# The first loads of x in contiguous rows, the first half block in two parts, and column pairs in the blocks of the first column quarter

## The chip, the core and the metric

The kernel runs on one NeuronCore of a Trainium2 chip. Its engines work side by side and are tied by semaphores: TensorE (PE) multiplies matrices, VectorE (DVE), ScalarE (ACT) and GpSimd (POOL) do elementwise work, and SyncE (SP) issues DMA transfers; ScalarE and GpSimd can issue some too. Sixteen DMA engines move the data. The metric is the device time of one execution in microseconds (us).

## The reference

Only the first of two sublayers matters here. `x` is 2048 x 512, the two sequence matrices are 2048 x 2048, all in float32.

```python
h = _layernorm(x, axis=-1) * (1 + ca) + sa
a = jnp.einsum("bsd,ed->bse", h, dft_hid_re)
b = jnp.einsum("bsd,ed->bse", h, dft_hid_im)
y = jnp.einsum("ts,bse->bte", dft_seq_re, a) - jnp.einsum("ts,bse->bte", dft_seq_im, b)
x = x + ga * y
```

The second sublayer (a gated MLP with a 2048 x 2048 spatial matrix `w_sp`) follows, and takes the rest of the time.

## The kernel before

**What is multiplied first.** The kernel begins with products of the sequence matrices (`cr`, `ci`) and the normalised rows of `x`. A matrix is taken in blocks of 512 x 512 (`quad`); `src` lists the 32 blocks in the order of use. A block has to be turned before TensorE can contract over its columns. It is loaded into a tile `stage[b]`, 128 partitions x 16 x 128, in four transfers, one for each 32 partitions (`load_block`), and VectorE turns it by 32 x 32 squares in four instructions (`squares`, k = 0 to 3), each of which gives a tile `t` of 128 x 512.

**Steps.** Step n = 4b + k uses turn k of block b and one row block of `x` (128 of its rows; rows "X[0]" to "X[3]" go with block 0). Products are made in pieces of high and low part: `ah` (ScalarE's rounded copy of `t`) and `al` (VectorE's difference `t` - `ah`) on one side, `hh` and `hl` of the normalised row on the other. A step is three groups of four matmuls: `ah` x `hh`, `al` x `hh`, `ah` x `hl`. Step 0 is an exception: four plain float32 matmuls of `t` with the whole normalised row `xn` (L543). `prep_hi` makes `t` and `ah`, `prep_lo` makes `al`; in the steady part `t` is made three steps ahead and `al` two.

**The rows of x.** `stats_first` makes mean and variance on VectorE (BN_STATS, BN_AGGR, an add), then GpSimd makes the power -1/2 and the product of mean and scale (for row 0 VectorE makes the product, L445). ScalarE then normalises: `whole_first` for row 0, `hi_first` for rows 1 to 3 (`hh`), `norm_x` once more for `xn`, from which VectorE subtracts `hh` (`lo_h`, L525).

**The order of the work** is written out by hand at the end of the function: every engine takes its instructions in the order of the code. The loads at the start are row 0 in four transfers (two queues, `two`), the first half of block 0 (columns 0 to 63 of each group of 128) in four, row 1 in four, rows 2 and 3 in four, the second half of block 0 in four, then block 1 and the next rows.

**Completion semaphores.** Each transfer that SyncE or ScalarE issues takes the next of eight completion semaphores (DMAHW0 to DMAHW7 in the rows of the order below), and its issue waits until the transfer that had this semaphore eight places before has landed. So at most eight are under way, and a queue that waits at one issue holds back all that stand behind it.

## Time and profile before

| | before |
|---|---|
| time, median of 3 runs (lowest to highest) | 931.72 us (931.36 to 932.32) |
| profiled execution: its time; its span | 931.77 us; 930.0 us |
| TensorE busy | 924.2 us, 99% of the span |
| VectorE, ScalarE, GpSimd busy | 738.2, 409.1, 199.1 us |
| TensorE's granted clock, mean | 0.999 |

The span goes from the first to the last instruction of the profiled execution; the time of the same execution is 1.77 us longer. A granted clock of 1 is full speed. An engine counts as busy while one of its instructions runs; waiting and issuing transfers don't count.

### The profile page before, as it was taken

How to read it: one execution, taken by the hardware profiler on the slowest of the kernel's cores; microseconds unless marked ns; L12 is line 12 of the kernel's file. 1: busy time of each engine (PE TensorE's matmuls, PEld its weight loads, DVE VectorE, ACT ScalarE, POOL GpSimd, SP SyncE). 2: the span in 40 equal slices, each digit the busy share in tenths (PEclk: the TensorE clock that was granted, in tenths of full speed). 3: DMA queues.
4: the chain of work that ended last, by engine and by line, in shares of the span. 5: the costliest groups of instructions: out<-in, count | busy, mean ns of one | idle time of the engine just before them, and what ended most of it. 6: DMA issues, size and time to landing. Idle time of an engine off the chain costs nothing.

```text
span 930.0 us, 12339 instructions
## 1 busy us (share of the span) xinstructions
PE 924.2 (99%) x4053; PEld 760.4 (82%) x4053; DVE 738.2 (79%) x1218; ACT 409.1 (44%) x733; POOL 199.1 (21%) x375
## 2 busy tenths in 40 slices
PE   9999999999999999999999999999999999999998
PEld 5888888888888888888888888888888888888887
DVE  7799968787687677875678788899799789986762
ACT  5694424232132222322577877674544544331121
POOL 2330000224554165323512321331000000000000
PEclk9999999999999999999999999999999999999999
DMA  9995762856639977996463864444464566734651
GB/s 218 225 227 118 142 158 46 193 147 171 158 91 319 283 220 217 275 343 227 141 217 130 279 201 103 118 105 105 105 146 102 130 142 143 178 97 149 185 178 57
DMA packets 246976, 157.88 MB, mean 170 GB/s; under 512 B 140384, under 2 KB 214368, under 8 KB 246784
## 3 DMA queue, kind: packets, MB, share of 16 engines
q1 hardware_dynamic: 233248, 119.57, 52.2%
q0 software_dynamic: 12272, 36.86, 11.4%
q8 instruction: 32, 0.52, 0.2%
q10 hardware_dynamic: 1392, 0.66, 0.2%
q14 instruction: 32, 0.26, 0.1%
HBM read 120.33 MB, written 36.71 MB: 169 GB/s over the span
## 4 chain that ended last, share of the span: by engine, by line
PE 98%; DMA 1%; SPq 0%; ACTq 0%; DVE 0%; ACT 0%; issue 0%; DVEq 0%
PE gp L99 12%; PE gp L97 12%; PE gp L98 12%; PE gw L99 10%; PE gw L97 10%; PE gw L98 10%; PE yp L99 3%; PE yp L98 3%; PE yp L97 3%; PE op L98 3%; PE op L97 3%; PE op L99 3%; PE fp L98 1%; PE fp L97 1%; PE fp L99 1%; PE z2s L98 1%
## 5 line engine op out<-in xcount | busy, mean ns | idle before, releaser
L269 ACT ACTIVATE ah<-t 128x512 fp32r<-128x512 f32 x235 | 148.5, 632 | 362.6 <-DVE t L190 242.7
L287 DVE TENSOR_TENSOR al<-t,ah 128x512 fp32r<-128x512 f32 x235 | 160.6, 683 | 55.7 <-PE gp L98 30.9
L98 PE MATMUL gp<-al,hh 128*128 128x512 f32 x496 | 193.0, 389 | 0.0
L97 PE MATMUL gp<-ah,hh 128*128 128x512 f32 x496 | 193.0, 389 | 0.0
L99 PE MATMUL gp<-ah,hl 128*128 128x512 f32 x496 | 193.0, 389 | 0.0
L190 DVE STREAM_TRANSPOSE t<-stage 128x512 f32<-128x512 f32 x236 | 165.5, 702 | 6.3 <-DMA stage<-in_A_dft_seq_re_dram 3.1
L98 PE MATMUL gw<-al,bh 128*128 128x512 f32 x400 | 155.6, 389 | 0.0
L99 PE MATMUL gw<-ah,bl 128*128 128x512 f32 x384 | 149.5, 389 | 0.0
L97 PE MATMUL gw<-ah,bh 128*128 128x512 f32 x384 | 149.4, 389 | 0.0
L98 PEld LDWEIGHTS gp<-al,hh 128*128 128x128 f32 x496 | 93.1, 188 | 19.5 <-DVE al L287 0.2
L97 PEld LDWEIGHTS gp<-ah,hh 128*128 128x128 f32 x496 | 93.1, 188 | 19.4
L99 PEld LDWEIGHTS gp<-ah,hl 128*128 128x128 f32 x496 | 93.1, 188 | 19.3
L98 PEld LDWEIGHTS gw<-al,bh 128*128 128x128 f32 x400 | 75.1, 188 | 15.7
L99 PEld LDWEIGHTS gw<-ah,bl 128*128 128x128 f32 x384 | 72.1, 188 | 15.3 <-DVE bl L948 0.3
L97 PEld LDWEIGHTS gw<-ah,bh 128*128 128x128 f32 x384 | 72.1, 188 | 14.9
L920 POOL DMA_DIRECT2D s_d<-sj x64 | 35.1, 548 | 107.2 <-DVE sj L912 82.3
L97 PE MATMUL yp<-hth,gh 128*128 128x512 f32 x128 | 49.8, 389 | 0.0
L98 PE MATMUL yp<-htl,gh 128*128 128x512 f32 x128 | 49.8, 389 | 0.0
L99 PE MATMUL yp<-hth,gl 128*128 128x512 f32 x128 | 49.8, 389 | 0.0
L665 POOL DMA_DIRECT2D ht_d<-hturn x62 | 41.0, 667 | 23.1 <-DVE hturn L661 18.2
L97 PE MATMUL op<-woh,uh 128*128 128x512 f32 x110 | 42.8, 389 | 0.0
L98 PE MATMUL op<-wol,uh 128*128 128x512 f32 x110 | 42.8, 389 | 0.0
(247 smaller groups left out, 1449.4 us busy)
## 6 DMA issues: line engine op xcount, KB each, us to landing
stage<-in_A_dft_seq_im_dram SPq DMA_DIRECT2D x64, 256.0 KB, 6.0
sj<-in_B_w_sp_dram SPq DMA_DIRECT2D x32, 512.0 KB, 7.2
s_d<-sj POOLq DMA_DIRECT2D x64, 256.0 KB, 4.7
stage<-s_d SPq DMA_DIRECT2D x128, 128.0 KB, 2.9
stage<-in_A_dft_seq_re_dram SPq DMA_DIRECT2D x60, 256.0 KB, 5.6
stage<-in_B_w_sp_dram SPq DMA_DIRECT2D x88, 128.0 KB, 3.0
wm<-in_w_mod_dram SPq DMA_DIRECT2D x16, 256.0 KB, 6.1
xr<-in_A_x_dram POOLq DMA_DIRECT2D x16, 256.0 KB, 4.5
```

What stands on the lines that cost most here:

```text
L97: nc.tensor.matmul(acc, ah, bh, start=first, stop=False, skip_group_check=go_on)
L98: nc.tensor.matmul(acc, ah, bl, start=False, stop=False, skip_group_check=go_on)
L99: nc.tensor.matmul(acc, al, bh, start=False, stop=last, skip_group_check=go_on)
L190: nc.vector.transpose(dst.rearrange("p (b i) -> p b i", i=32), block[:, :, 32 * k:32 * k + 32])
L269: nc.scalar.activation(AH[n], T[n], AF.Copy)
L287: nc.vector.tensor_tensor(AL[n], t, AH[n].bitcast(F32), op=ALU.subtract)
L665: eng.dma_start(v[a, i], ht[32 * a:32 * a + 32].rearrange("c (b r) -> c b r", r=32))
L920: nc.gpsimd.dma_start(s_d[m, r, g][b * P:(b + 1) * P, :], a)
```

## The change

Row blocks 0 and 1 now are the first 256 rows of `x` (each group of 32 partitions has 64 rows running), and row blocks 2 and 3 are the next 256, two neighbouring rows for each partition, so that they come in one transfer of 128 x 1024. The blocks of the first column quarter of `cr` and `ci` (eight of the 32, `SRC_G` 0) are loaded to match: `load_pairs` takes 64 columns at a time, so each of these blocks but the first takes eight transfers where it took four, in runs of 64 elements where there were 128. `turn_dft` turns k = 0 and 1 as before; for k = 2 and 3 it reads every second element, since the columns of the two row blocks alternate.

The first half of block 0 comes in two parts, twelve squares and four squares, each in four transfers, and is turned for step 0 in the same two parts. Both parts stand ahead of row 1, of which ScalarE issues one transfer, after its table load and first activation, and SyncE three. The normalising of row 0 and the high part of row 1 are made in halves of 256 columns. GpSimd makes row 0's product of mean and scale. VectorE takes the statistics of row 1 ahead of the turn for step 1.

```diff
@@ -133,11 +133,12 @@
     def quad(a, r, k):
         return a[r * Q:(r + 1) * Q, k * Q:(k + 1) * Q]
 
-    src = []
+    src, SRC_G = [], []
     for t in range(NQ):
         for g, j in ([(g, j) for g in range(NQ) for j in range(2)] if t == 0 else
                      [(g, j) for j in range(2) for g in range(NQ)]):
             src.append(quad((cr, ci)[j], t, g))
+            SRC_G.append(g)
     N2 = 4 * len(src)
     N1 = N2 + 8
     YPROD = (6, 7, 4, 5, 3)
@@ -160,12 +161,31 @@
         for q in range(4):
             engs[q].dma_start(tile_[32 * q:32 * q + 32], v[q][:, :, 64 * h:64 * h + 64])
 
+    def load_pairs(tile_, a, h, engs=(nc.sync,) * 4, bs=slice(0, 16)):
+
+        v = a.rearrange("(b j) (h a s) -> h a j b s", j=32, a=4, h=2)
+        for q in range(4):
+            engs[q].dma_start(tile_[32 * q:32 * q + 32, bs, 64 * h:64 * h + 64], v[h, q][:, bs, :])
+
+    def turn_dft(n, block, k, bs=slice(0, 16)):
+
+        t = T[n].rearrange("p (b i) -> p b i", i=32)
+        if SRC_G[n // 4] or k < 2:
+            nc.vector.transpose(t[:, bs, :], block[:, bs, 32 * k:32 * k + 32])
+        else:
+            v = block.rearrange("p b (h i c) -> p b h i c", h=2, c=2)
+            nc.vector.transpose(t[:, bs, :], v[:, bs, 1, :, k - 2])
+
     XB = []
 
     def load(b):
         if b < len(src):
             stage[b] = blocks.tile([P, 16, P], F32, tag="stage", bufs=2, name=f"stage{b}")
-            load_block(stage[b], src[b])
+            if SRC_G[b]:
+                load_block(stage[b], src[b])
+            else:
+                for h in range(2):
+                    load_pairs(stage[b], src[b], h)
         elif b < len(src) + 2:
             j = b - len(src)
             XB.append(blocks.tile([P, 4, Q], F32, tag="stage", bufs=2, name=f"xb{j}"))
@@ -264,7 +284,7 @@
             elif n >= N4:
                 squares(T[n], stage[b][:, k % 2], k // 2)
             else:
-                squares(T[n], stage[b], k)
+                turn_dft(n, stage[b], k)
         AH[n] = SE[2][:, n - N4] if N4 <= n < N4 + 4 else blocks.tile([P, Q], F32R, tag="ah", bufs=4, name=f"ah{n}")
         nc.scalar.activation(AH[n], T[n], AF.Copy)
         if not N2 <= n < N4 and k == 3:
@@ -365,8 +385,8 @@
     def keep_busy(n, k):
 
         ps = bank(k, "busyp")
-        for _ in range(n):
-            nc.tensor.matmul(ps, ones, busy, start=True, stop=True)
+        for w in n:
+            nc.tensor.matmul(ps[:, :w], ones, busy[:, :w], start=True, stop=True)
 
     def fold_sum(t, w, u):
 
@@ -419,14 +439,18 @@
 
     X, XG, LN, NRM, h_hi, h_lo = {}, {}, {}, {}, {}, {}
 
-    def load_x(g, ks=range(4), eng=nc.sync):
+    def load_x(g, ks=range(4), engs=(nc.sync,) * 4):
 
         if g not in XG:
             XG[g] = spool.tile([P, 4, D], F32, tag="x", bufs=2, name=f"x{g}")
         k0, k1 = ks[0], ks[-1] + 1
-        v = x.rearrange("(g a k i) d -> g a i k d", g=NQ, a=4, i=32)
-        for a in range(4):
-            eng.dma_start(XG[g][32 * a:32 * a + 32, k0:k1, :], v[g, a][:, k0:k1, :])
+        if not g and k0 == 2:
+            nc.sync.dma_start(XG[g][:, 2:, :], x[2 * P:Q, :].rearrange("(p k) d -> p k d", k=2))
+        else:
+            v = (x.rearrange("(g a k i) d -> g a i k d", g=NQ, a=4, i=32)[g] if g else
+                 x[:2 * P, :].rearrange("(a k i) d -> a i k d", a=4, i=32))
+            for a in range(4):
+                engs[a].dma_start(XG[g][32 * a:32 * a + 32, k0:k1, :], v[a][:, k0:k1, :])
         for k in ks:
             X[4 * g + k] = XG[g][:, k, :]
 
@@ -435,32 +459,34 @@
 
     def stats_first(s):
 
-        m = spool.tile([P, 12], F32, tag="first", bufs=4, name=f"first{s}")
-        nc.vector.bn_stats(m[:, :6], X[s])
-        mv = m[:, 8:]
-        nc.vector.bn_aggr(mv[:, :2], m[:, :6])
+        sums_first(s)
+        norm_first(s)
+
+    def sums_first(s):
+        M1[s] = spool.tile([P, 12], F32, tag="first", bufs=4, name=f"first{s}")
+        nc.vector.bn_stats(M1[s][:, :6], X[s])
+
+    def norm_first(s):
+
+        mv = M1[s][:, 8:]
+        nc.vector.bn_aggr(mv[:, :2], M1[s][:, :6])
         nc.vector.tensor_scalar(mv[:, 1:2], mv[:, 1:2], EPS, None, op0=ALU.add)
         nc.gpsimd.tensor_tensor(mv[:, 2:3], mv[:, 1:2], mhalf, op=ALU.pow)
-        eng = nc.gpsimd if s else nc.vector
-        eng.tensor_scalar(mv[:, 3:4], mv[:, 0:1], mv[:, 2:3], -1.0, op0=ALU.mult, op1=ALU.mult)
+        nc.gpsimd.tensor_scalar(mv[:, 3:4], mv[:, 0:1], mv[:, 2:3], -1.0, op0=ALU.mult, op1=ALU.mult)
         NRM[s] = mv[:, 2:3], mv[:, 3:4]
 
-    two = (nc.sync, nc.sync, nc.scalar, nc.scalar)
-
-    def load_two(k):
-        if not k:
-            XG[0] = spool.tile([P, 4, D], F32, tag="x", bufs=2, name="x0")
-        v = x.rearrange("(g a k i) d -> g a i k d", g=NQ, a=4, i=32)
-        for a in range(4):
-            two[a].dma_start(XG[0][32 * a:32 * a + 32, k, :], v[0, a][:, k, :])
-        X[k] = XG[0][:, k, :]
+    M1 = {}
+
+    def halves(h, s):
+
+        v = X[s].rearrange("p (a k i) -> p k a i", a=4, i=32)
+        for ks in (slice(1, 3), slice(0, 4, 3)):
+            nc.scalar.activation(h[:, ks], v[:, ks], AF.Identity, bias=NRM[s][1], scale=NRM[s][0])
 
     def whole_first(s):
 
         LN[s] = spool.tile([P, D], F32, tag="xn", bufs=4, name=f"xn{s}")
-        nc.scalar.activation(LN[s].rearrange("p (k a i) -> p k a i", a=4, i=32),
-                             X[s].rearrange("p (a k i) -> p k a i", a=4, i=32), AF.Identity,
-                             bias=NRM[s][1], scale=NRM[s][0])
+        halves(LN[s].rearrange("p (k a i) -> p k a i", a=4, i=32), s)
         nc.scalar.activation(LN[s][:, :1], ones[:, :1], AF.Copy)
 
     def split_first(s):
@@ -473,15 +499,19 @@
 
     def turn_whole(n):
         T[n] = blocks.tile([P, Q], F32, tag="t", bufs=2, name=f"t{n}")
-        squares(T[n], stage[0], n)
+        for bs in PARTS:
+            turn_dft(n, stage[0], n, bs)
         highs.add(n)
         lows.add(n)
 
     def hi_first(s):
         h_hi[s] = hpool.tile([P, ND, P], F32R, name=f"hh{s}")
         h = h_hi[s].rearrange("p k (a i) -> p k a i", i=32)
-        nc.scalar.activation(h, X[s].rearrange("p (a k i) -> p k a i", a=4, i=32), AF.Identity,
-                             bias=NRM[s][1], scale=NRM[s][0])
+        if s == 1:
+            halves(h, s)
+        else:
+            nc.scalar.activation(h, X[s].rearrange("p (a k i) -> p k a i", a=4, i=32), AF.Identity,
+                                 bias=NRM[s][1], scale=NRM[s][0])
         nc.scalar.activation(h_hi[s][:, 0, :1], ones[:, :1], AF.Copy)
 
     def sum_x(s):
@@ -1084,26 +1114,29 @@
             mm([n])
 
 
-    load_two(0)
+    PARTS = (slice(0, 12), slice(12, 16))
+    two = (nc.sync, nc.sync, nc.scalar, nc.scalar)
+    load_x(0, range(1), two)
     stage[0] = blocks.tile([P, 16, P], F32, tag="stage", bufs=2, name="stage0")
-    load_half(stage[0][:, :, :64], src[0], 0, two)
-    load_two(1)
+    for bs in PARTS:
+        load_pairs(stage[0], src[0], 0, two, bs)
     nc.scalar.activation(sc, ones[:, :ND], AF.Silu)
+    load_x(0, range(1, 2), (nc.sync,) * 3 + (nc.scalar,))
     load_x(0, range(2, 4))
-    load_half(stage[0][:, :, 64:], src[0], 1)
+    load_pairs(stage[0], src[0], 1)
     load(1)
     load_x(1, range(2))
-    keep_busy(3, 5)
+    keep_busy((Q, Q, Q), 5)
     ones_x(1)
     ones_x(2)
     ones_x(3)
     stats_first(0)
     whole_first(0)
     turn_whole(0)
+    stats_first(1)
     prep_hi(1)
-    stats_first(1)
+    hi_first(1)
     prep_lo(1)
-    hi_first(1)
     stats_first(2)
     norm_x(1)
     stats_first(3)
```

**SyncE at the start.** x_138 holds row blocks 0 to 3, stage_143 is block 0, stage_161 block 1 (after: stage_162). Before:

```order
L455 DMA x_138<-in_A_x_dram 32x512 x2
L161 DMA stage_143<-in_A_dft_seq_re_dram 32x16x64 x2
L455 DMA x_138<-in_A_x_dram 32x512 [waits DMAHW1_49]
L455 DMA x_138<-in_A_x_dram 32x512 [waits DMAHW3_49]
L429 DMA x_138<-in_A_x_dram 32x2x512 [waits DMAHW4_49]
L429 DMA x_138<-in_A_x_dram 32x2x512 [waits DMAHW5_49]
L429 DMA x_138<-in_A_x_dram 32x2x512 [waits DMAHW6_49]
L429 DMA x_138<-in_A_x_dram 32x2x512 [waits DMAHW7_49]
L161 DMA stage_143<-in_A_dft_seq_re_dram 32x16x64 [waits DMAHW0_49]
L161 DMA stage_143<-in_A_dft_seq_re_dram 32x16x64 [waits DMAHW1_49]
L161 DMA stage_143<-in_A_dft_seq_re_dram 32x16x64 [waits DMAHW2_49]
L161 DMA stage_143<-in_A_dft_seq_re_dram 32x16x64 [waits DMAHW3_49]
```

After:

```order
L453 DMA x_138<-in_A_x_dram 32x512 x2
L168 DMA stage_143<-in_A_dft_seq_re_dram 32x12x64 x2
L168 DMA stage_143<-in_A_dft_seq_re_dram 32x4x64 [waits DMAHW1_49]
L168 DMA stage_143<-in_A_dft_seq_re_dram 32x4x64 [waits DMAHW3_49]
L453 DMA x_138<-in_A_x_dram 32x512 [waits DMAHW4_49]
L453 DMA x_138<-in_A_x_dram 32x512 [waits DMAHW5_49]
L453 DMA x_138<-in_A_x_dram 32x512 [waits DMAHW7_49]
L448 DMA x_138<-in_A_x_dram 128x1024 [waits DMAHW0_49]
L168 DMA stage_143<-in_A_dft_seq_re_dram 32x16x64 [waits DMAHW1_49]
L168 DMA stage_143<-in_A_dft_seq_re_dram 32x16x64 [waits DMAHW2_49]
L168 DMA stage_143<-in_A_dft_seq_re_dram 32x16x64 [waits DMAHW3_49]
L168 DMA stage_143<-in_A_dft_seq_re_dram 32x16x64 [waits DMAHW4_49]
```

The second half of block 0 still stands ninth to twelfth, but the part of four squares has come in front of row 1, and row 1's transfers now wait for those of the twelve squares (DMAHW4, 5 and 7); rows 2 and 3 have become one.

**ScalarE at the start.** xn is the normalised row, hh the high part of a row. Before:

```order
L455 DMA x_138<-in_A_x_dram 32x512 x2
L161 DMA stage_143<-in_A_dft_seq_re_dram 32x16x64 x2
L455 DMA x_138<-in_A_x_dram 32x512 [waits DMAHW0_49]
L455 DMA x_138<-in_A_x_dram 32x512 [waits DMAHW2_49]
L1091 ACT_TABLE_LOAD
L1091 ACTIVATE sc<-ones 128x4 [waits Pool_49]
L461 ACTIVATE xn_187<-x_138,first_181 128x512 [waits DMAHW3_49,DMAHW1_49,DVE_49]
L464 ACTIVATE xn_187<-ones 128x1 [waits Activation_49]
L269 ACTIVATE ah_194<-t_192 128x512 [waits DVE_49]
L483 ACTIVATE hh_204<-x_138,first_196 128x512 [waits DMAHW2_49,DMAHW1_49,DMAHW3_49,DMAHW0_49,Pool_49]
```

After:

```order
L453 DMA x_138<-in_A_x_dram 32x512 x2
L168 DMA stage_143<-in_A_dft_seq_re_dram 32x12x64 x2
L168 DMA stage_143<-in_A_dft_seq_re_dram 32x4x64 [waits DMAHW0_49]
L168 DMA stage_143<-in_A_dft_seq_re_dram 32x4x64 [waits DMAHW2_49]
L1123 ACT_TABLE_LOAD
L1123 ACTIVATE sc<-ones 128x4 [waits Pool_49]
L453 DMA x_138<-in_A_x_dram 32x512 [waits DMAHW6_49]
L484 ACTIVATE xn_192<-x_138,first_186 128x256 [waits DMAHW3_49,DMAHW1_49,Pool_49]
L484 ACTIVATE xn_192<-x_138,first_186 128x2x128
L490 ACTIVATE xn_192<-ones 128x1 [waits Activation_49]
L289 ACTIVATE ah_207<-t_205 128x512 [waits DVE_49]
L484 ACTIVATE hh_209<-x_138,first_199 128x256 [waits DMAHW6_49,DMAHW5_49,DMAHW7_49,DMAHW4_49,Pool_49]
```

ScalarE's two transfers of row 1 have become one, which stands behind the activation that loads the table and waits for ScalarE's second transfer of the twelve squares (DMAHW6).

**VectorE at the start.** t_190 and t_192 are the turns for steps 0 and 1 (after: t_196 and t_205), t_225 (t_233) that for step 2. Before:

```order
L445 TENSOR_SCALAR first_181<-first_181 128x1 [waits Pool_49]
L190 STREAM_TRANSPOSE t_190<-stage_143 128x512 [waits DMAHW6_49,DMAHW7_49,DMAHW5_49,DMAHW4_49]
L190 STREAM_TRANSPOSE t_192<-stage_143 128x512
L439 BN_STATS first_196<-x_138 128x6 [waits DMAHW2_49,DMAHW3_49,DMAHW1_49,DMAHW0_49]
L441 BN_AGGR first_196<-first_196 128x2 [waits DVE_49]
L442 TENSOR_SCALAR first_196<-first_196 128x1 [waits DVE_49]
L287 TENSOR_TENSOR al_202<-t_192,ah_194 128x512 [waits Activation_49]
L439 BN_STATS first_207<-x_138 128x6 [waits DMAHW6_49,DMAHW7_49,DMAHW5_49,DMAHW4_49]
L441 BN_AGGR first_207<-first_207 128x2 [waits DVE_49]
L442 TENSOR_SCALAR first_207<-first_207 128x1 [waits DVE_49]
L439 BN_STATS first_214<-x_138 128x6
L441 BN_AGGR first_214<-first_214 128x2 [waits DVE_49]
```

After:

```order
L174 STREAM_TRANSPOSE t_196<-stage_143 128x384 [waits DMAHW6_49,DMAHW7_49,DMAHW5_49,DMAHW4_49]
L174 STREAM_TRANSPOSE t_196<-stage_143 128x128 [waits DMAHW2_49,DMAHW3_49,DMAHW1_49,DMAHW0_49]
L467 BN_STATS first_199<-x_138 128x6 [waits DMAHW6_49,DMAHW7_49,DMAHW5_49,DMAHW4_49]
L472 BN_AGGR first_199<-first_199 128x2 [waits DVE_49]
L473 TENSOR_SCALAR first_199<-first_199 128x1 [waits DVE_49]
L174 STREAM_TRANSPOSE t_205<-stage_143 128x512
L307 TENSOR_TENSOR al_213<-t_205,ah_207 128x512 [waits Activation_49]
L467 BN_STATS first_215<-x_138 128x6 [waits DMAHW0_49]
L472 BN_AGGR first_215<-first_215 128x2 [waits DVE_49]
L473 TENSOR_SCALAR first_215<-first_215 128x1 [waits DVE_49]
L467 BN_STATS first_222<-x_138 128x6
L472 BN_AGGR first_222<-first_222 128x2 [waits DVE_49]
```

The statistics of row 1 now stand in front of the turn for step 1, and the small product of row 0 has left VectorE.

## Rows read from the trace of the kernel before

**Rows 1.** Busy time by engine, one long stretch (us and instructions, clock, DMA share, GB/s).
```profile
14.26:925.00 910.74, 910.74 (x4017) 753.52 (x4018) 728.79 (x1196) 401.94 (x721) 194.65 (x359) 1.00 0.64 170
```

**Rows 2.** Waits of TensorE's weight loads, whole run: total us, times, longest.
```profile
PEld gp L549 <- ACT ah L269: 1.1, 1, 1.1
PEld gp L549 <- ACT hh L483: 0.7, 1, 0.7
```

**Rows 3.** Chain that ended last, its beginning: start us, us, what.
```profile
2.12 3.64 DMA stage<-in_A_dft_seq_re_dram
...
8.40 4.31 DMA stage<-in_A_dft_seq_re_dram
12.83 0.72 DVE t L190
13.57 0.64 ACT ah L269
```

**Rows 4.** Timeline, SyncE's queue and ScalarE: start us, us, what, idle time and its releaser.
```profile
4.84 1.98 SPq L429 DMA_DIRECT2D x<-in_A_x_dram  x4
...
5.32 0.20 ACT L1091 ACTIVATE sc<-ones 128x4 f32<-128x4 f32 x1
```

**Rows 5.** Waits of SyncE's queue, first 35 us: total us, times, longest.
```profile
SPq L429 <- DMA stage<-in_A_dft_seq_re_dram: 1.0, 1, 1.0
```

**Rows 6.** Landing of the first four loads of x.
```profile
DMA to landing us min/median/max: 2.0/2.2/2.5
```

**Rows 7.** Landing of the second four loads of x.
```profile
DMA to landing us min/median/max: 3.0/3.1/3.3
```

**Rows 8.** Timeline, the other engines up to the third step.
```profile
5.10 0.55 POOL L443 TENSOR_TENSOR first<-first,mhalf 128x1 f32<-128x1 f32 x1 [4.03 <-DVE first L442]
...
5.93 0.81 ACT L461 ACTIVATE xn<-x,first 128x512 f32<-128x512 f32 x1 [0.41 <-DVE first L445]
5.96 1.30 DVE L190 STREAM_TRANSPOSE t<-stage 128x512 f32<-128x512 f32 x2
...
6.82 3.85 PE L543 MATMUL gp<-t,xn 128*128 128x512 f32 x8
...
7.19 0.65 DVE L439 BATCH_NORM_STATS2 first<-x 128x6 f32<-128x512 f32 x1
...
8.16 0.68 DVE L287 TENSOR_TENSOR al<-t,ah 128x512 fp32r<-128x512 f32 x1
...
9.31 0.69 DVE L439 BATCH_NORM_STATS2 first<-x 128x6 f32<-128x512 f32 x1 [0.47 <-DMA x<-in_A_x_dram]
9.36 0.27 POOL L445 TENSOR_SCALAR first<-first 128x1 f32<-128x1 f32 x1
...
10.33 0.68 DVE L439 BATCH_NORM_STATS2 first<-x 128x6 f32<-128x512 f32 x1
...
11.45 0.69 DVE L525 TENSOR_TENSOR hl<-xn,hh 128x512 fp32r<-128x512 f32 x1
```

**Rows 9.** DMA view, 624 to 628 us.
```profile
DMA packets 3599, 0.90 MB, mean 226 GB/s; under 512 B 3598, under 2 KB 3598, under 8 KB 3598
```

**Rows 10.** DMA view, 34 to 38 us.
```profile
DMA packets 1605, 0.90 MB, mean 226 GB/s; under 512 B 60, under 2 KB 1535, under 8 KB 1604
```

**Rows 11.** Timeline, VectorE, 40 to 53 us.
```profile
46.10 0.71 DVE L190 STREAM_TRANSPOSE t<-stage 128x512 f32<-128x512 f32 x1 [2.36 <-DMA stage<-in_A_dft_seq_re_dram]
46.73 0.65 DVE L287 TENSOR_TENSOR al<-t,ah 128x512 fp32r<-128x512 f32 x1
```

**Rows 12.** Timeline, TensorE, around 50 us.
```profile
50.03 0.39 PE L98 MATMUL gp<-al,hh 128*128 128x512 f32 x1
```

**Rows 13.** Timeline, VectorE, 145 to 163 us.
```profile
153.15 0.70 DVE L190 STREAM_TRANSPOSE t<-stage 128x512 f32<-128x512 f32 x1
...
160.77 0.65 DVE L287 TENSOR_TENSOR al<-t,ah 128x512 fp32r<-128x512 f32 x1
```

**Rows 14.** Timeline, TensorE, around 161 us.
```profile
161.55 0.42 PE L98 MATMUL gp<-al,hh 128*128 128x512 f32 x1
```

## The prediction

> **What bounds the kernel now.** I read the busy times by stretch first. From 14.26 us, the start of step 2, to 925 us TensorE is busy for 910.74 of 910.74 us at the full clock [rows 1]. What happens behind step 2 therefore costs nothing as long as it stays hidden, and whatever moves the start of step 2 moves the end of the kernel by as much. Ahead of it, the waits of the weight loads show the only two places with something to win: 0.7 us ahead of step 1, for the high part of row 1 (`hh`), and 1.1 us ahead of step 2, for `ah` [rows 2]. The beginning of the chain of waits shows what stands behind the second: a transfer of the second half of block 0, issued at 8.40 and landed 4.31 us later, VectorE's turn at 12.83 to 13.55 and ScalarE's copy to 14.21 [rows 3]. So the turn for step 2 ends at 13.55 and the question is when it ends afterwards.
>
> VectorE works in the order of the code, and the reader is to see in its timeline that it had time to spare: it turned for steps 0 and 1 at 5.96, took the statistics of row 1 at 7.19, and then waited 0.47 us for rows 2 and 3 ahead of 9.31 [rows 8]. Before, then, the loads set the start of step 2, and VectorE didn't.
>
> **The change part by part.**
>
> *Rows 2 and 3 in one transfer.* SyncE issues one where it issued four. The second half of block 0 stands behind it in the queue, so its four issues, the last at 8.40 before, come earlier: four issues took 1.98 us [rows 4], so three fewer save 1.5 and would put the last at 6.9. But what stands ahead of them now waits longer (next part), and I take 1 us of that back: 7.9. With the same 4.31 us it lands at about 12.2 and allows a turn at 12.3, 0.5 us earlier than now. This is all that the loads can give unless they also land faster.
>
> *Row 1 behind both parts of the half block.* This is the costly edit. Every issue waits for the transfer eight places before it; the first transfer of rows 2 and 3 lost 1.0 us in this way, waiting for the half block [rows 5]. Before, the place eight ahead of row 1 was row 0, landed early. Now it is the part of twelve squares. The half block's last transfer landed at 2.12 + 3.64 = 5.76 [rows 3]; without the quarter that now comes later I put the end of the twelve squares at 5.3, an estimate that takes a quarter off some 2 us of data. ScalarE's transfer of row 1 can't be issued ahead of that. If it also waits for the activation in front of it, which ended at 5.52 [rows 4], it goes out at about 5.5. Row 0's loads, into empty queues, landed 2.0 to 2.5 us after their issue, median 2.2 [rows 6]; row 1's, behind others, 3.0 to 3.3 [rows 7]. Few bytes are ahead of it now, so I take 2.2: row 1 is there at 7.7, with 5.3 + 2.0 = 7.3 and 5.5 + 3.3 = 8.8 as the ends.
>
> *Statistics of row 1 ahead of the turn for step 1.* The turn, and all that VectorE does up to step 2, now queue behind row 1. From the start S of the statistics to the end of the turn for step 2, by rows: statistics up to the next instruction 0.97 (7.19 to 8.16), the turn for step 1 0.65 (half of 1.30), `ah` 0.64, `al` 0.68, the statistics of rows 2 and 3 1.02 and 1.12 (9.31 to 10.33 to 11.45), `hl` 0.69, the turn 0.72 [rows 3, 8]. That is 6.49, and I take S + 6.5; handovers to ScalarE and the overlap of neighbours on VectorE about cancel. The break-even is S = 13.55 - 6.5 = 7.05. With S = 7.7 the turn ends at 14.2, 0.65 us later than now, and the 0.5 us that the loads gained are covered. VectorE idles from about 6.3 (the turn for step 0 done) to 7.7: that is the wait which takes the place of the old ones. Step 2's `ah` and matmuls wait behind it, and so does everything after.
>
> *Halves and the product on GpSimd.* The power ends at 5.65, and the product on GpSimd costs 0.27 where VectorE had the scale and shift ready for ScalarE at 5.93 [rows 8]; ScalarE starts at about 6.05. A half of the 0.81 us activation lies between 0.41 and 0.81; with 0.20 of fixed part, as the four-column activation costs [rows 4, 8], it is 0.5. Step 0 could start at 6.6 instead of 6.82, and the two parts of its turn, started at 5.3, are done by then. The 0.2 us are lost again ahead of step 1: its `hh` needs row 1's statistics and now also stands behind `ah`, so its first half ends at S + 0.97 + 0.65 + 0.64 + 0.5 plus handovers, about 10.6, which is where step 0's matmuls end in the row (6.82 + 3.85 = 10.67): step 1 begins about where it did. Step 1 lasts longer than before, because its third group waits for `hl`, but step 2 waits longer still. Cost beyond the above: nothing. The second halves add about 0.2 us each to ScalarE ahead of a wait.
>
> *Eight blocks in runs of 64 elements.* Seven blocks more take eight issues instead of four. The second half of the run already does so: 256 byte runs gave 226 GB/s over 624 to 628 us, as much as 512 byte runs over 34 to 38 us [rows 9, 10]. I cost this at nothing. The cover where it is thinnest: VectorE waited 2.36 us for a block at 46.10, and the `al` behind it ended at 47.38, 2.65 us ahead of its matmul at 50.03 [rows 11, 12].
>
> *Every second element in sixteen turns.* No row has such a read. I take the 0.7 us of a turn; the bounds are 0 and, if each element cost twice, some 0.5 us more for each (0.7 less a fixed 0.2). The Trainium skill ("SBUF — State Buffer", section "Door 1: The DMA port swizzle") says that reads keep full bandwidth with two or more hits in a 16 byte line, which these have, so by it the cost is nothing; no run here shows that yet.
>
> **Sum.** The profiled execution took 931.77 us (span 930.0). The end of the turn for step 2 moves from 13.55 to 14.2: +0.65, rounded to +0.6. 931.77 + 0.6 = 932.4; the median of the runs is 0.05 below the profiled one, so **932.3 us**. With row 1 at 7.3 to 8.2 the addition is +0.2 to +1.2, so the forecast's own range is 931.9 to 932.9. What a measurement can't tell from no change is 0.2%, 1.86 us: from 929.9 to 933.6.
>
> **Rivals.**
> 1. *Row 1 is in time* (faster). If its loads land by 6.3, when the turn for step 0 is done, S + 6.5 = 12.8, the turn for step 2 ends 0.75 us earlier, and the second half of block 0 at 12.2 allows it: 931.0. It decides for a gain as soon as S is below 7.05. For it: the issues are fewer, and 2 us from issue to landing is possible [rows 6]. Against it: the wait for the twelve squares, which can't end much before 5.3.
> 2. *Nothing moves* (within 0.2 us): S happens to lie near 7.05, or the gain of the earlier second half is what is seen. 931.7. For it, that both shifts are small and opposite.
> 3. *Short runs cost double* (slower). Block 1, 1 MB, is loaded while the queues are full from 8 us on. At the 226 GB/s of [rows 10] it takes 4.6 us; at half the rate all loads behind it come 4.6 us later, and `al` at 47.38 misses its matmul by 4.6 - 2.65 - 0.6 = 1.3 us: 932.3 + 1.3 = 933.6. The Trainium skill ("DMA: Bandwidth & Descriptors", section "Specifications") states that line rate wants transfers of 512 bytes or more. By that rule this edit costs; the trace disagrees as far as [rows 9, 10] go.
> 4. *Strided turns cost double* (slower). Step 2's turn ends 0.5 us later. In the third block that is read so, the turn at 153.15 stands in an unbroken run of VectorE ahead of an `al` that ends at 161.42, 0.13 us ahead of its matmul at 161.55 [rows 13, 14]: another 0.4 us. Together +0.9, 933.2; with a second place as tight, it passes 933.6.
>
> **How the numbers follow.** Forecast (+0.2 to +1.2): 0.60. Rival 1: 0.18. Rival 2: 0.10. Rivals 3 and 4: 0.06 each. Only the slow ends of 3 and 4 and a row 1 much later than 8.8 leave the band upwards, 0.07. Downwards there is no case but row 1 in time together with a second half that lands a further microsecond earlier, 0.03. The rest, 0.90, is within 0.2%. The range takes in rival 1 at its end and the forecast with the bound of S, 930.9 to 933.4.
>
> **What would show it.** Right: statistics of row 1 at 7.3 to 8.2 after an idle VectorE, released by a transfer of x; the second half of block 0 landed while VectorE is still at row 2, 3 or `hl`; the turn for step 2 without a wait for a transfer; step 2 at about 14.9; TensorE without a gap behind it. Wrong: statistics of row 1 ahead of 7.05, or the turn for step 2 again released by a transfer; turns of every second element longer than 0.75 us; a gap of TensorE near 50 or 161 us. The forecast fails first at the time at which the twelve squares land, since each 0.1 us there is 0.1 us at the end.

## The result, and the profile after

| | before | changed |
|---|---|---|
| median of 22 runs each (lowest to highest) | 931.61 us (930.99 to 932.32) | 933.26 us (932.3 to 935.92) |
| ratio, 95% interval | | 1.0023 [1.0017, 1.0029] |
| profiled execution: its time; its span | 931.77 us; 930.0 us | 932.84 us; 931.0 us |

The median, 933.26 us, lies just inside the range (930.9 to 933.4); the mean of the 22, 933.76, lies outside it. The forecast was "within 0.2%", with a chance of 0.90, and the kernel became slower by 0.23%: that is the distance of the means (933.76 to 931.58), while the medians are 0.18% apart. Of the 22 runs seven have a mean granted clock of 0.998 and take 934.59 to 935.92 us; the other fifteen are at 0.999 or 1.0, 932.3 to 934.4 us with a median of 932.89, which is 0.14% above before. None of the runs of before that were made beside the experiments is listed below 0.999. So there are two things to explain: 1.3 us in the usual execution, and another 2.3 us in a third of them (the mean of the seven is 935.33, of the fifteen 933.02). The 2.3 us lie between the first and the last instruction, since time less span is 1.8 to 1.9 us in all 22.

Between the start and 925 us nothing is lost in the profiled execution. The busy time by stretch (us; then PE, PEld, DVE, ACT, POOL, clock, DMA share, GB/s) of the changed kernel, to be held against [rows 1]:

```profile
16.00:925.00 909.00, 909.00 (x4010) 752.17 (x4009) 728.39 (x1195) 401.05 (x720) 194.92 (x359) 1.00 0.64 170
```

The chain that ended last now begins so, in place of [rows 3] (start us, us, what):

```profile
1.66 2.92 DMA stage<-in_A_dft_seq_re_dram
4.60 0.32 SPq L453
4.96 0.42 SPq L453
5.43 2.44 DMA x<-in_A_x_dram
7.99 0.70 DVE first L467
9.09 0.63 DVE t L174
9.74 0.64 ACT ah L289
10.40 0.69 DVE al L307
11.10 0.61 DVE first L467
12.10 0.61 DVE first L467
13.20 0.45 issue
13.65 0.72 DVE t L177
14.39 0.64 ACT ah L289
15.07 5.74 PE gp L579 x24
```

The reader is to see a chain that before went from a transfer of the second half of block 0 straight into the turn for step 2, and now goes through row 1: a transfer of the twelve squares lands at 4.58, SyncE's issues of row 1 wait for it and its fellows, row 1 lands at 7.87, and from there on VectorE works without a stop, but for 0.7 us in which it waits for ScalarE's `ah`, until the turn for step 2, which ends at 14.37 where it ended at 13.55. Step 2 starts at 15.07, before at 14.26. VectorE's timeline shows the idle time that this costs (timeline, VectorE, to be held against [rows 8]):

```profile
7.99 0.69 DVE L467 BATCH_NORM_STATS2 first<-x 128x6 f32<-128x512 f32 x1 [1.30 <-DMA x<-in_A_x_dram]
...
11.02 0.69 DVE L467 BATCH_NORM_STATS2 first<-x 128x6 f32<-128x512 f32 x1
...
13.65 1.30 DVE L177 STREAM_TRANSPOSE t<-stage 128x512 f32<-128x512 f32 x2
```

SyncE's queue in the timeline, for [rows 4]:

```profile
4.60 1.25 SPq L453 DMA_DIRECT2D x<-in_A_x_dram  x3
5.89 0.42 SPq L448 DMA_DIRECT2D x<-in_A_x_dram  x1
6.36 2.02 SPq L168 DMA_DIRECT2D stage<-in_A_dft_seq_re_dram  x4
```

Rows 2 and 3 are issued at 5.89, where their first of four stood at 4.84 before. TensorE's timeline shows three waits up to step 2 where before there was one; first the one of before, then the timeline of the changed kernel:

```profile
14.26 1.20 PE L549 MATMUL gp<-ah,hh 128*128 128x512 f32 x4 [0.72 <-ACT ah L269]
```

```profile
6.84 3.67 PE L573 MATMUL gp<-t,xn 128*128 128x512 f32 x8 [1.05 <-DVE t L174]
10.92 1.23 PE L579 MATMUL gp<-ah,hh 128*128 128x512 f32 x4 [0.40 <-ACT hh L484]
...
13.78 1.21 PE L579 MATMUL gp<-ah,hl 128*128 128x512 f32 x4 [0.72 <-DVE hl L555]
15.07 1.19 PE L579 MATMUL gp<-ah,hh 128*128 128x512 f32 x4
```

The wait ahead of step 0 differs between executions: in five of the ten profiles that there are of this kernel it is missing, in the others it takes 0.2 to 1.15 us.

### The profile page after: what moved, and what is told of

Read it like the earlier page. It is cut to its first block, busy times and chain, and to the rows that moved or that the text cites. A ratio compares the mean times of both kernels' runs of the same rounds, so it can differ in the third digit from the quotient of the medians.

```text
span 931.0 us, 12386 instructions
## 1 busy us (share of the span) xinstructions
PE 923.5 (99%) x4053; PEld 760.0 (82%) x4053; DVE 738.6 (79%) x1218; ACT 409.6 (44%) x735; POOL 199.1 (21%) x376
## 4 chain that ended last, share of the span: by engine, by line
PE 98%; DVE 1%; DMA 1%; ACT 0%; issue 0%; ACTq 0%; SPq 0%; DVEq 0%
PE gp L99 12%; PE gp L97 12%; PE gp L98 12%; PE gw L98 10%; PE gw L99 10%; PE gw L97 10%; PE yp L99 3%; PE yp L98 3%; PE yp L97 3%; PE op L97 3%; PE op L98 3%; PE op L99 3%; PE fp L98 1%; PE fp L99 1%; PE fp L97 1%; PE z2s L98 1%
## 5 line engine op out<-in xcount | busy, mean ns | idle before, releaser
L174 DVE STREAM_TRANSPOSE t<-stage 128x512 f32<-128x512 f32 (+1 forms) x113 | 78.4, 695 | 5.4 <-DMA stage<-in_A_dft_seq_re_dram 3.3
L210 DVE STREAM_TRANSPOSE t<-stage 128x512 f32<-128x512 f32 x108 | 76.2, 706 | 2.5 <-DMA stage<-in_B_w_sp_dram 1.5
```

Source lines behind the costliest of these rows:

```text
L174: nc.vector.transpose(t[:, bs, :], block[:, bs, 32 * k:32 * k + 32])
L210: nc.vector.transpose(dst.rearrange("p (b i) -> p b i", i=32), block[:, :, 32 * k:32 * k + 32])
```

## The experiments

Theory A: row 1's loads, which wait for the twelve squares, set the start S of row 1's statistics, and S sets step 2. Rival B: the short runs or the strided turns cost. Rival C: the second half of block 0, or its transfers, still set step 2. Rival D, formed on the way: the one transfer of rows 2 and 3. The late executions near 935 us are a question of their own; the guess is TensorE's clock, because TensorE now waits ahead of step 0. Each median stands beside that of the kernel before, timed on the same chip; the ratio and its interval follow in brackets.

**The changed kernel again** (no edit), timed:

> The changed kernel once more, beside the others on one chip. Theory A (row 1 comes late by its wait, and besides that some executions lose TensorE's clock for a while near the start, because TensorE idles more there): most executions near 932.8 us with a mean clock of 0.999 or 1.000, about a third near 935.3 with a mean clock of 0.998. If the profile is one of the slow third, its granted clock falls to half somewhere in the first 20 us and step 2 starts later than 15.1 us, or the matmuls behind it take longer. Rival B (short runs or strided reads cost something later in the kernel): the slow third shows gaps of TensorE later than 20 us at full clock.

932.56 us beside 931.36 (1.0016 [1.0007, 1.0024]); one run of eleven, 935.2 us, had clock 0.998, where a third was expected. In the profile S is 7.51, earlier by 0.48, but VectorE waited once more, for the transfer of rows 2 and 3, issued at 5.85 and landed at 11.01, and step 2 starts at 15.09.

```profile
11.03 0.69 DVE L467 BATCH_NORM_STATS2 first<-x 128x6 f32<-128x512 f32 x1 [0.41 <-DMA x<-in_A_x_dram]
```

**The half block in one part, row 1 ahead of ScalarE's table load**: everything else of the change stays.

```diff
-    PARTS = (slice(0, 12), slice(12, 16))
+    PARTS = (slice(0, 16),)
...
+    load_x(0, range(1, 2), two)
     nc.scalar.activation(sc, ones[:, :ND], AF.Silu)
-    load_x(0, range(1, 2), (nc.sync,) * 3 + (nc.scalar,))
```

> The first half block in one part again, and row 1 in two transfers on each queue ahead of the table load, so that its issues wait for row 0 as before; data layout, paired columns, halves, the one transfer for rows 2 and 3 and the order on VectorE stay as changed. Theory A: row 1's statistics start at 6.7 to 7.0, the turn for step 2 ends at 13.2 to 13.5, and the time is 931.2 to 931.7, that is 0.2 to 0.4 below the kernel before, with few or no executions near 935. Rival B: 932.5 or more, and the slow third stays, since all short runs and strided reads are still there.

931.98 us beside 931.36 (1.0009 [1.0, 1.0018]). S is 6.84 and step 2 follows at 13.92 (timeline, VectorE):

```profile
6.84 0.69 DVE L467 BATCH_NORM_STATS2 first<-x 128x6 f32<-128x512 f32 x1 [0.18 <-DMA x<-in_A_x_dram]
...
12.50 1.30 DVE L177 STREAM_TRANSPOSE t<-stage 128x512 f32<-128x512 f32 x2
```

Row 1 comes 1.15 us earlier than in the changed profile, and step 2 by the same 1.15. That is theory A; and since all short runs and strided turns are still in this kernel, B doesn't explain those 1.15 us. The expected time was missed: not 0.2 to 0.4 us below before, but 0.62 above. Of the 0.62, 0.35 lie outside the span (time less span is 2.13 us, and 1.78 in before), for which no theory here has a reason; the median spans are 929.9 and 929.5. The rest can go with the base of the expectation, which was one profile of before (below, "The sum").

**More work to keep TensorE busy ahead of step 0** (`keep_busy((Q, Q, Q, Q // 2, Q // 4), 5)`), for the late executions:

> The changed kernel with two more of the matmuls that keep TensorE busy ahead of step 0 (256 and 128 columns). They fill the idle 1.05 us between the third of them and step 0; the loads and VectorE are as changed. Theory A with the gap ahead of step 0 as the cause of the lost clock: no execution near 935, all within 932.3 to 933.5, so the median falls by about 0.5 to 932.7. Theory A with the gaps inside and behind step 1 as the cause: the slow third stays. Rival B: the slow third stays.

932.53 us (1.0012 [1.0003, 1.0021]), no run at 0.998. Step 0 starts at 7.18 without a wait, and step 2 at 15.07 as in the changed kernel: the wait ahead of step 0 as such costs nothing in the usual execution. Of the late ones it tells nothing, since the unchanged kernel too had a series of eleven without any (below).

**The kernel before with less of it** (`keep_busy(2, 5)`):

> The kernel before with two instead of three of these matmuls, nothing else, so that TensorE idles 1 to 2 us longer ahead of step 0. Theory A with the gap ahead of step 0 as the cause: some executions now end 2 to 3.5 us later at a mean clock of 0.998, the others at 931.6 as before. With the gaps in step 1 as the cause, or by rival B: all at 931.6 (931.0 to 932.3).

932.31 us (1.0007 [0.9999, 1.0016]). Its profiled execution, 932.45 us, lost time at the start (timeline, TensorE):

```profile
6.85 5.51 PE L543 MATMUL gp<-t,xn 128*128 128x512 f32 x8 [1.57 <-DVE t L190]
11.80 1.48 PE L549 MATMUL gp<-ah,hh 128*128 128x512 f32 x4
```

Step 0's eight matmuls take 5.51 us where they took 3.85 in [rows 8], behind a wait of 1.57 us that the kernel before doesn't have. Step 2 starts at 14.95. The trace's records of the clock begin only at 10.57 in this execution, so that its listed mean of 1.0 says nothing of step 0. But step 0's matmuls start 0.85 to 0.98 us apart up to 10.39, and 0.43 us apart from 10.91 on. The expectation came half true: one run of eleven is 2.3 us above before's median (933.7, listed at 1.0), and the one that is listed at 0.998 took 932.45 us. The same trace holds a second thing, since its loads are those of before: the turn for step 2 starts 0.37 us earlier than in [rows 3].

```profile
12.46 1.31 DVE L190 STREAM_TRANSPOSE t<-stage 128x512 f32<-128x512 f32 x2 [0.28 <-DMA stage<-in_A_dft_seq_re_dram]
```

**The changed kernel with less of it** (`keep_busy((Q, Q), 5)`):

> The changed kernel with two instead of three of the matmuls that keep TensorE busy ahead of step 0. Theory A with the gap ahead of step 0 as the cause of the late executions: the late kind (935 and more, clock 0.998) becomes frequent, half of the executions or more, and the median rises to 934 to 936; if the profiled execution is of that kind, the granted clock reaches full speed only behind 8 us and step 0's eight passes stand 0.85 us apart instead of 0.43. Rival (the late kind comes from something later in the kernel): the same mixture as the changed kernel, median 932.5 to 933.3.

932.6 us (1.0014 [1.0005, 1.0022]); one run of eleven at 0.998, of 932.73 us. The wait ahead of step 0 grew to 1.50 us, step 0 took 3.67 all the same, and no run was near 935. The expectation failed: a longer wait there didn't make the late executions frequent. And a mean of 0.998 needn't cost 2 us, as its run of 932.73 shows.

**The old order on VectorE** (the turn for step 1 again ahead of row 1's statistics):

```diff
-    stats_first(1)
     prep_hi(1)
-    hi_first(1)
+    stats_first(1)
     prep_lo(1)
+    hi_first(1)
```

> The changed kernel with the turn for step 1 ahead of row 1's statistics again, as before; loads, parts and halves as changed. Theory A (VectorE's chain from row 1's statistics sets step 2): the chain loses the turn (0.65) and the wait for ah (0.64), so the turn for step 2 ends at about 13.3 to 13.6 instead of 14.4, or later only if the transfer of rows 2 and 3 holds it; median of the executions without late clock 931.5 to 931.9. Rival C (the second half of block 0, or its transfers, set step 2): the turn for step 2 stays at 14.2 or more and is released by a transfer, and the time stays at 932.5.

932.33 us (1.0012 [1.0003, 1.0021]), no better than the changed kernel. The chain says why (start us, us, what):

```profile
5.88 4.95 DMA x<-in_A_x_dram
10.85 0.70 DVE first L467
...
13.49 0.71 DVE t L177
```

With the turn out of the way the transfer of rows 2 and 3 takes over: issued at 5.88, it takes 4.95 us, and step 2 starts at 14.91. The expected times failed: the expectation named this exception and gave it no price. Rival C falls here, since the turn follows VectorE's own work, and the second half of block 0 had landed at 12.36.

**Row 1 right behind row 0**, ahead of the half block, its statistics ahead of the turn for step 0:

```diff
     load_x(0, range(1), two)
+    load_x(0, range(1, 2), two)
...
     nc.scalar.activation(sc, ones[:, :ND], AF.Silu)
-    load_x(0, range(1, 2), (nc.sync,) * 3 + (nc.scalar,))
...
-    turn_whole(0)
     stats_first(1)
+    turn_whole(0)
```

> The changed kernel with row 1's four loads right behind row 0's, two on each queue, and row 1's statistics ahead of step 0's turn; the half block in its two parts behind them. Theory A (row 1's wait for the twelve squares sets S): statistics of row 1 start at 4.7 to 5.5, the turn for step 2 ends at 12.6 to 13.2 and step 2 starts at 13.4 to 13.9, against 15.1; step 0 starts later, at 7.2 to 7.6, since 256 KB go ahead of the half block. Time 931.0 to 931.7 for executions without late clock; the gap of TensorE ahead of step 0 grows, so some late ones are likely. Rival C: step 2 stays at 15 or is released by a transfer.

932.29 us (1.0011 [1.0002, 1.002]): five runs at 931.72 to 931.89, four at 932.29 to 932.99 with a clock of 1.0, and two at a clock of 0.998 or less, 933.57 and 933.78. The expectation (931.0 to 931.7) was missed even by the five: S is 5.00, as expected, but step 0 starts at 8.25 and the turn for step 2 at 12.90, 7.9 us behind S, with waits for the half block and for rows 2 and 3 between. The profile is of the last one, at 0.997 (timeline, TensorE):

```profile
8.25 5.37 PE L573 MATMUL gp<-t,xn 128*128 128x512 f32 x8 [2.13 <-DVE t L174]
13.06 1.49 PE L579 MATMUL gp<-ah,hh 128*128 128x512 f32 x4
```

and its busy times by stretch give a granted clock of one half behind that wait:

```profile
9.00:11.00 2.00, 2.00 (x4) 0.97 (x3) 1.40 (x3) 1.97 (x5) 0.00 (x0) 0.50 1.03 225
```

TensorE waited 2.13 us and then ran at 1.2 GHz through a part of step 0, which took 5.37 us instead of 3.67. Step 2 started at 16.21, and the run took 1.9 us more than the five without such a loss.

**Layouts and loads of the change alone**: one part, row 1 ahead of the table load, VectorE in the old order, `hh` of row 1 whole (the edits of the one-part and old-order kernels, and `if True:` for `if s == 1:` in `hi_first`):

> The kernel of the one part (e2) with the old order on VectorE and row 1's high part in one piece, so that of the change the data layout, the paired columns, the one transfer for rows 2 and 3, the halves of row 0 and GpSimd's product are left. Theory A: VectorE waits for hl of row 1, the turn for step 2 ends at 12.5 to 13.0, 0.2 to 0.7 earlier than in the kernel before, and the time is 930.8 to 931.3, not later than the kernel before. Rival B (short runs and strided reads cost): 932 or more.

931.65 us beside 931.18 (1.0005 [0.9996, 1.0014]). S is 7.13, rows 2 and 3 landed at 9.35, step 2 starts at 13.49. This kernel has the pairs of columns, the strided turns and the single transfer, and can't be told from before: the median spans are 929.5 and 929.4. The expected time (930.8 to 931.3) was missed by 0.35 us; 0.33 us more than in before lie outside the span here too.

**Old order, and rows 2 and 3 in four transfers**, against D:

```diff
-            nc.sync.dma_start(XG[g][:, 2:, :], x[2 * P:Q, :].rearrange("(p k) d -> p k d", k=2))
+            for a in range(4):
+                nc.sync.dma_start(XG[g][32 * a:32 * a + 32, 2:, :], x[2 * P + 64 * a:2 * P + 64 * a + 64, :].rearrange("(p k) d -> p k d", k=2))
```

> The kernel with the old order on VectorE (e6) and rows 2 and 3 in four transfers of 128 KB again (the same rows, 32 partitions each). In e6 the statistics of row 2 were released at 10.85 by the one transfer, which landed 4.9 us after its issue. Theory D (the one transfer lands late and sets step 2 together with row 1): the four land by 9.6 to 10.2, the turn for step 2 ends at 13.0 to 13.6 instead of 14.2, and the median falls from 932.3 to 931.6 to 932.0. Rival (what is late is the issue, behind row 1's waits, and the bytes take as long in four): rows 2 and 3 land at 10.6 or later and the time stays at 932.3.

932.37 us (1.0013 [1.0004, 1.0022]). The four are issued from 5.65 on and the last lands at 9.71, 4.06 us after the first issue, where the one took 4.95 in the old-order kernel:

```profile
9.83 0.69 DVE L468 BATCH_NORM_STATS2 first<-x 128x6 f32<-128x512 f32 x1 [0.83 <-DMA x<-in_A_x_dram]
```

Step 2 starts at 13.99 in this profile, as D expects, 0.37 of the 0.9 us because S is earlier (7.31 against 7.68). But the times didn't follow: 932.37 against 932.33. In this execution 0.5 us more pass from step 2 to the end of the span than in before (916.25 against 915.74): 0.15 up to the last matmul, in the products of `w_sp` (below), and 0.37 behind it. D is shown as a wait of VectorE, and not as time.

**Layouts and loads alone, rows 2 and 3 in four** (both edits above):

> The kernel of e8 (half block in one part, row 1 with two on each queue, old order on VectorE) with rows 2 and 3 in four transfers. Theory D: they land at 8.6 to 9.0 instead of 9.35, VectorE's statistics of row 2 start at 8.9 to 9.0, step 2 at 13.2 to 13.5; time 931.2 to 931.6, equal to the kernel before or up to 0.3 below e8. Rival: no difference from e8 (931.65), or later, since the second half of block 0 is issued three issues later.

931.46 us beside 931.16 (1.0001 [0.9992, 1.001]): as before, and in the expected range. Rows 2 and 3 landed at 8.81, against 9.35 in the kernel with one transfer, but step 2 starts no earlier (13.63, expected 13.2 to 13.5), since VectorE then waits 0.56 us for `xn`. No version here beats the kernel before.

**The changed kernel unchanged, for more profiles**, and once timed:

> The changed kernel once more for a profile; about one execution in four is of the late kind. If this one is (934.4 to 936): the granted clock falls to half for some 3.4 us within the first 20 us, or reaches full speed that much later, and the matmuls in that stretch stand at twice the distance; step 2 starts at 17 or later. If it is not: as the profile of the changed kernel, step 2 at 14.7 to 15.1.

> As the look before: a late execution shows half the clock in a stretch of the first 20 us and step 2 at 17 or later, another one step 2 at 14.7 to 15.1.

> The changed kernel once more, unchanged, for one profiled execution. Theory (the clock is lost at the start in some executions): most of these four executions take 932.3 to 933.3 us, with step 2 at 14.7 to 15.1; where one takes 934 us or more, its mean granted clock is 0.998 or lower, a stretch at half clock lies between 5 and 16 us behind one of TensorE's waits ahead of steps 0 to 2, and step 2 begins at 16.5 or later. Rival (the time is lost elsewhere): in an execution of 934 us or more step 2 begins by 15.3, and the gap or the half clock lies behind 16 us, or outside the span.

> As for the look before: theory, 932.3 to 933.3 us with step 2 at 14.7 to 15.1, or 934 us and more with half clock between 5 and 16 us and step 2 at 16.5 or later; rival, 934 us and more with step 2 by 15.3.

> As for the looks before: theory, 932.3 to 933.3 us with step 2 at 14.7 to 15.1, or 934 us and more with half clock between 5 and 16 us and step 2 at 16.5 or later; rival, 934 us and more with step 2 by 15.3.

> As for the looks before: theory, 932.3 to 933.3 us with step 2 at 14.7 to 15.1, or 934 us and more with half clock between 5 and 16 us and step 2 at 16.5 or later; rival, 934 us and more with step 2 by 15.3.

> The changed kernel unchanged, timed again. If executions of 934.4 us and more belong to the kernel, 1 to 4 of 11 are of that kind at a mean clock of 0.998 and the median is 932.5 to 933.0; if they belonged to the first comparison's chip or moment, none is, and the median is 932.3 to 932.8. Profiled execution: end of the turn for step 2 at the start of row 1's statistics plus 6.36 us, or later if rows 2 and 3 land behind 10.7.

> The changed kernel unchanged: 932.3 to 933.3 us with step 2 at 14.3 to 15.5; or 934 us and more, then with half clock between 5 and 16 us and step 2 at 16.5 or later (rival: 934 us and more with step 2 by 15.5).

In this order: 932.49, 932.87, 932.60, 932.64, 933.69 and 932.83 us; then the timed one with 932.43 us beside 931.09 (1.0013 [1.0004, 1.0022]), its profiled execution at 932.39; then 932.49. No run of the timed one is at 0.998, and none of the profiled ones is of the late kind. By the expectation of the timed one that speaks for the chip or the moment of the first comparison; the one late run in the repeat speaks against that as the whole answer. Two executions fell outside what was expected, 932.60 with step 2 as early as 14.35, and 933.69 with step 2 at 15.50. With the two profiles above there are ten of one kernel, and they test theory A without any edit (in order of S; the last column is the end of the turn for step 2 less S):

| profiled time | S | turn for step 2 ends | step 2 | less S |
|---|---|---|---|---|
| 932.60 | 7.27 | 13.63 | 14.35 | 6.36 |
| 932.39 | 7.51 | 13.87 | 14.59 | 6.36 |
| 932.84 (first repeat) | 7.51 | 14.37 | 15.09 | 6.86 |
| 932.49 | 7.60 | 13.96 | 14.68 | 6.36 |
| 932.49 | 7.67 | 14.03 | 14.74 | 6.36 |
| 932.64 | 7.68 | 14.04 | 14.76 | 6.36 |
| 932.87 | 7.70 | 14.36 | 15.08 | 6.66 |
| 932.83 | 7.95 | 14.31 | 15.03 | 6.36 |
| 932.84 (shown above) | 7.99 | 14.35 | 15.07 | 6.36 |
| 933.69 | 8.43 | 14.78 | 15.50 | 6.35 |

The last one is the same chain with a transfer of row 1 that took longer:

```profile
5.22 3.09 DMA x<-in_A_x_dram
8.43 0.70 DVE first L467
...
14.08 0.71 DVE t L177
```

In eight of ten the turn ends 6.35 or 6.36 us after S, whatever S is. In the other two (6.86, 6.66) VectorE also waited for rows 2 and 3, which landed at 11.01 and 10.99; the theory's own sum doesn't have that wait. And from step 2 to the last matmul it takes 912.19 to 912.25 us in seven of the ten, 912.32 in one and 912.65 and 912.70 in two, against 912.20 in before: what moves step 2 moves the end of TensorE's work by as much.

## Why the prediction was right or wrong, by its steps

**Row 1's wait.** Right, in mechanism and size. S was put at 7.7 with 7.3 to 8.8 as the ends: the ten profiles give 7.27 to 8.43, mean 7.73. "S + 6.5" is S + 6.36 when nothing else waits. Step 2 was put at 14.9; the mean of the ten is 14.89, 0.63 us behind before's profile, for a forecast of 0.65. (The 0.7 and 1.1 us of [rows 2] are waits of the weight loads; the matmuls themselves waited only once, 0.72 us ahead of step 2.)

**Rows 2 and 3 in one transfer.** Half right. It does free the second half of block 0, whose last issue came at 7.89 (forecast 7.9) and which landed by 12.10 (forecast 12.2), and the turn for step 2 waits for no transfer. The microsecond by which row 1's waits delay the issues was in the sum, but only for the second half. Not foreseen: rows 2 and 3 themselves land at 9.6 to 11.0, where they can hold the statistics of row 2, in two of ten profiles by 0.3 and 0.5 us.

**Step 0 and step 1.** "Step 0 could start at 6.6 ... step 1 begins about where it did": it started at 6.84 and 10.92 in the profile shown. This costs nothing in itself, since step 2 waits longer still, but the change opened waits of TensorE at the start, and the prediction asked nothing about them.

**Short runs and strided turns** (rivals 3 and 4). Both fell. The costliest groups show the strided turns (L177) beside the plain ones (count | busy us, mean ns | idle us before):

```profile
L174 DVE STREAM_TRANSPOSE t<-stage 128x512 f32<-128x512 f32 x111 | 77.5, 699 | 4.3 <-DMA stage<-in_A_dft_seq_re_dram 2.4 <-DMA stage<-in_A_dft_seq_im_dram 1.0
L177 DVE STREAM_TRANSPOSE t<-stage 128x512 f32<-128x512 f32 x16 | 11.2, 703 | 0.1
```

703 ns against 699: the rule cited from the Trainium skill ("SBUF — State Buffer", section "Door 1: The DMA port swizzle") holds here. And TensorE has no gap in the stretch from 16 to 925 us, so the runs of 256 bytes stay hidden; whether such a transfer takes longer by itself is not shown.

**The sum.** The step that failed here is the addition, "+0.65, rounded to +0.6": the usual execution loses 1.2 to 1.3 us (the fifteen 932.89 against 931.61, the repeats 932.56 against 931.36 and 932.43 against 931.09), twice as much. The chain that it follows is right; its distance from before was mis-sized. The 13.55 for before's turn comes from one profiled execution, of 931.77 us and a span of 930.0. The medians of before in the comparisons since are 931.61, 931.36, 931.18, 931.16 and 931.09, so that profile was 0.2 to 0.7 us above the usual time; the median spans beside the experiments are 929.3 to 929.5. The trace of the kernel before with less busy work fits that: with the same loads its turn starts at 12.46 instead of 12.83. That before's usual step 2 is as much earlier is inferred from the spans, since there is only this one profile of before.

On the other side the mean of the ten profiled times is 932.77, 0.37 above the 932.4 of the sum. "Cost beyond the above: nothing" doesn't hold: on average 0.27 us more pass between step 2 and the end of the span (916.01 against 915.74). Of these, the part behind the last matmul is 3.67 to 3.70 us in all ten, against 3.53 in before; why it grew by 0.15 us stays open. The last matmul of before, and that of the changed kernel (timeline, TensorE; the spans end at 930.00 and 930.96):

```profile
926.18 0.28 PE L99 MATMUL last<-woh,ul 128*128 128x256 f32 x1
```

```profile
927.00 0.28 PE L99 MATMUL last<-woh,ul 128*128 128x256 f32 x1
```

The rest of the 0.27 is in the products of `w_sp` (last section), and another 0.1 us lies outside the span.

**The chances.** This addition alone leaves the usual execution inside the band, as forecast (1.0016 and 1.0013 in the repeats). The step that failed and took the result out of it is "only the slow ends of 3 and 4 and a row 1 much later than 8.8 leave the band upwards, 0.07". What left it were the seven runs at 0.998: without them the mean of the 22 is 933.02 instead of 933.76, so they carry 0.73 us, 0.08%, of the 0.23%. The prediction put a case of lower clock at nothing, without a reason.

What makes these runs stays open. They came in 7 of 22 runs, then in 1 of 11, 0 of 11 and none of seven single executions, and no profile caught one. The listed mean says something, though. In the profile shown its 0.999 comes from the end of the program, when TensorE has nothing left to do (busy time by stretch):

```profile
929.50:930.90 1.40, 0.00 (x0) 0.00 (x0) 0.00 (x0) 0.00 (x0) 0.00 (x0) 0.50 0.02 6
```

There the clock is at one half for the last 1.5 us, and in none of the ten profiles for longer. A mean of 0.998 over 933 us stands for 2.8 to 4.7 us at one half (an estimate, from the rounding of 0.998), so another such stretch in these runs is likely. At the most that is 1.4 to 2.3 us of lost work, the upper end of which would do for the 2.3 us; but where the stretch lies was not seen. In two other kernels a step 0 that runs long behind a wait of TensorE was seen (waits of 1.57 and 2.13 us; the granted clock of one half is in the rows of the second). For the changed kernel it is only argued, and there is a number against the simplest form: a step 0 that takes 1.7 to 1.8 us longer would be covered in part by the 0.40 and 0.72 us of waits behind it, and leave some 0.7, not 2.3. If it is the clock, it must be lost in, or last into, what stands behind those waits.

## What to carry to other kernels

Where an issue waits for the transfer eight places ahead, a load that is put in front of another decides when that other one starts: count the places along the queue, for every load behind it. And make a sum of tenths of a microsecond against many timed executions, not against the one that was profiled: here the base alone was off by up to as much as the effect. If a change opens waits of TensorE at the start of a kernel, give a case of its own to executions at a lower mean clock.

## What the runs showed of the hardware

One transfer of 128 x 1024 against four of 32 x 1024 for the same rows: in the two pairs of kernels that differ only by this the one took 4.95 and 4.61 us from issue to landing, the four 4.06 and 4.14 us from the first issue to the last landing. That is one profile of each; in the ten profiles of the changed kernel the one took 3.6 to 5.2 us, so which is faster is not shown. The four weren't slower.

The second place where TensorE runs close is far behind the change. In two of the ten profiles (932.60 and 933.69) the last stretch of the program comes 0.3 to 0.5 us later relative to step 2 than in the others; it is a block of `w_sp` that VectorE waited for, and TensorE behind it (timeline of the first of them, TensorE):

```profile
807.47 0.50 PE L99 MATMUL gw<-ah,bl 128*128 128x512 f32 x1 [0.17 <-DVE bl L978]
```

It comes and goes between executions of the same program. The two have the earliest and the latest step 2 of the ten (14.35 and 15.50), so it doesn't follow from the start; it scatters the times by as much as a change of the start is worth.
